# Weight sums on GpSimd, stores through SyncE and conversions at other hooks, in a three-layer kernel on one core

## The chip, the cores and the metric

The kernel runs on one core of a Trainium2 chip. The metric is the device time of one execution in microseconds; less is better. TensorE (PE in the profile) multiplies matrices, VectorE (DVE), ScalarE (ACT) and GpSimd (POOL) work on elements, and SyncE (SP) issues transfers. Each engine runs its own instructions in program order, and semaphores order the engines among each other.

## The reference, cut to what matters

```python
q_s = softmax(q, axis=-1); k_s = softmax(k, axis=2)       # (4, 8, 576, 64)
kv = einsum('bhsd,bhse->bhde', k_s, v)
x = einsum('bhsd,bhde->bhse', q_s, kv)                    # reshaped to (2304, 512)
p = domain_probs / (domain_probs.sum(-1) + 1e-09)         # (2304, 4)
y = sum(p[:, e:e+1] * (relu(x @ w1[e]) @ w2[e]) for e in range(4))   # w1 512x1024, w2 1024x512
h = y @ w_in                                              # 512x2048, float64 in memory
out = elu(h) @ w_out                                      # 2048x512, float64 in memory
```

The outputs are float32. The weights of the last layer arrive as float64.

## The kernel before, in words

The kernel has one long list of matmuls for TensorE, and puts the work of the other engines between them by hand. A matrix product keeps float32 accuracy by splitting each operand in a high and a low part (`hi`, `lo`) and adding three products.

**Stages.** First comes attention for 16 pairs of heads, interleaved from about 23 us on with the first expert (`first`, `second`, matmuls of line 974). From about 272 us the remaining work goes in 30 `STEPS` (s, b): s counts groups of four 128-wide blocks of the hidden layer, b the three blocks of 768 tokens. Steps with s < 6 belong to experts 1 to 3, steps with s from 6 on to the last layer with its ELU. In each step the first layer is done by seven products of sums of quarters instead of eight (`product`, line 1110, twice seven a step). The operands on the token side (`ring_load`, line 688) come from memory through eight ring slots. A slot is loaded in the second half of a step and read in the first half of the next. For s < 5 the second layer is done the same way (`second_product`, line 1254); later steps use plain matmuls (`chunk`, lines 1167 to 1169).

**Weight parts.** Every step group needs two calls of `w1_steps(s, p)`. Each turns a raw weight tile `r` into four pairs of high and low parts: `hi(k)` is a copy on ScalarE (line 734), `lo(k)` a subtraction on VectorE (line 744). `sums1` (lines 748 and 749) and `sums2` (lines 753 and 754) overwrite the raw tile with the sums that later parts need, on VectorE. The order is begin with `hi(0)`, `lo(0)`, `sums1`, `hi(1)`, `lo(1)`, `sums2`, `hi(2)`, `lo(2)`, `hi(3)`, `lo(3)`. There are 20 such parts: two ahead of the first step, then in the last step of one group and the first of the next. When `lo(3)` is done, the buffer of `r` is free for the next weight load (`w_load`).

**Conversions.** `convert` turns one tile of a float64 weight into float32 in 32 runs. The load is issued on SyncE (lines 435 and 437), then come lines 455, 461 and 465 on VectorE, an exponential on ScalarE (468), lines 471 and 474 on VectorE, and the store to a scratch tensor in memory (477), issued on ScalarE. Runs marked `aside` use the tile `gt`, which the fast steps use as well. `w_load` reads the scratch tensor in the last layer.

**Hooks.** What is put between matmuls hangs on numbered hooks. Up to 272 us a hook comes after every 2048 columns of line 974 and runs what `at(n, fn)` put there; before hook 0 the list `START` gives the order by name. In the steps there are 24 hooks a step (`at2`, `tick`), run between products. A conversion at hook t has its load at t - 7 and its instructions at the offsets of its list, spaced 2 (d = 2) or 1 (d = 1).

**Steps behind a product.** After product 0 of a half step ScalarE copies one bank (line 1312), after product 1 another (1314); after products 2 and 4 VectorE adds (1319, 1326). Line 1276 adds a second-layer product to the accumulator. In the ELU steps ScalarE runs lines 1140 to 1142, VectorE 1143 and 1145, ScalarE 1149 and GpSimd 1150. The domain weights `pn` are normalised by `normalise` (lines 605 to 608), four VectorE operations at hook 2; `pn` is first read when expert 0 leaves PSUM (line 1017).

```python
for s, (put, t, d, aside) in enumerate(CONV):
    put(t - 7, lambda s=s, x=aside: convert_load(s, x))
    for n, fn in zip((0, 1, 2, 3, 4, 5, 7) if d == 1 else (0, 2, 4, 6, 10, 12, 16), convert(s, aside)):
        put(t + n, fn)
```

Of the kernel before, what the change touches and what calls it, by code (L numbers as in the profile page):

```python
# [21 lines left out]
def tile_attention_moe_moe(  # L22
# [13 lines left out]
    nc = tc.nc  # L36
# [19 lines left out]
        kvlo2 qmul2 qturn1 x0 qhi1 kcopy3 qturn2 xhi0 qlo1 qhi2 x1 whi1 xhi1 krec3 xlo0 wlo0 qlo2 qturn3 kv3  # L56
        xlo1 qhi3 qlo3 x2 kvhi3 wlo1 xhi2 kvlo3 x3 xhi3 xlo2 xlo3 p0 p1
    """
# [381 lines left out]
    def convert(s, aside):  # L440
# [35 lines left out]
        )  # L476
        yield lambda: nc.scalar.dma_start(out=scratch[s // 2, :, s % 2, :], in_=t["y"])

# [132 lines left out]

    at(2, normalise)

# [101 lines left out]
    def w1_steps(s, p):  # L715
# [27 lines left out]
        def lo(k):  # L743
            tt(out=dst(k, 1), in0=src(k), in1=dst(k, 0).bitcast(F32), op=ALU.subtract)  # L744

# [5 lines left out]
        def sums2():  # L751
            f1, f2 = r[0][:, 0], r[0][:, 1]
            tt(out=f2[:, 2:], in0=f2[:, 2:], in1=f1[:, :2], op=ALU.subtract)
            tt(out=f1[:, 2:], in0=f1[:, 2:], in1=f2[:, 2:], op=ALU.subtract)

        m = int(s >= S_MOE)
        return {
            -5: begin, -4: lambda: lo(0), -2: sums1, -1: lambda: hi(1), 0: lambda: lo(1), 1: sums2,
            4: lambda: hi(2), 5: lambda: lo(2), 8: lambda: hi(3), 10 - m: lambda: lo(3),
        }  # L760
# [72 lines left out]
    end1 = NB * S_FAST * SH  # L833
    CONV = [(at, t, 2, True) for t in (12, 30, 48, 146, 164)]
    CONV += [(later, 34 + 22 * n, 2, False) for n in range(15)]
    CONV += [(later, end1 + 13 + 12 * n, 1, True) for n in range(3)]
    end2 = NB * S_MOE * SH
    CONV += [(later, end2 + 40 + 12 * n, 1, True) for n in range(NCONV - len(CONV))]
    for s, (put, t, d, aside) in enumerate(CONV):
        put(t - 7, lambda s=s, x=aside: convert_load(s, x))  # L840
        for n, fn in zip((0, 1, 2, 3, 4, 5, 7) if d == 1 else (0, 2, 4, 6, 10, 12, 16), convert(s, aside)):
            put(t + n, fn)
# [202 lines left out]
    for step in START.split():  # L1045
        n, i = step[:-1], int(step[-1])
        if n == "whi":
            whi(0, i)
        elif n == "wlo":
            wlo_ahead(0, i)  # L1050
        elif n == "p":
            hidden(0, 0, (i,), 0, EARLY_D)
        elif n == "l":
            early_loads()
        elif n in K_STEPS:
            K_STEPS[n](i, lambda s: bank(early[s]))
        else:
            Q_STEPS[n](i, lambda s: bank(early[s]), (0,))
# [362 lines left out]
```

## Time and profile before

| | us |
|---|---|
| median of 3 runs | 1239.99 (1238.53 to 1240.53) |
| the profiled execution | 1239.69 |
| its span, first to last instruction | 1237.9 |
| TensorE busy | 1194.2 (96%) |
| VectorE busy | 846.2 (68%) |
| ScalarE busy | 635.4 (51%) |
| GpSimd busy | 511.3 (41%) |

The times of the engines are unions of their instructions' spans. Matmuls are pipelined, so a busy TensorE isn't always at its peak. In timelines a number in brackets is the idle time of the engine just before the instruction, with what ended it. "ACTq" and "SPq" are DMA issues by ScalarE's and SyncE's sequencers, not counted as busy. PEclk is the granted TensorE clock as a share of 2.4 GHz; 0.5 is 1.2 GHz.

### The profile page before, as it was taken

To read this page: it belongs to the slowest core of one execution; us is meant where nothing else is said; L and a number is where in the kernel's file an instruction comes from. 1 tells how busy PE (TensorE), PEld (TensorE's weight loads), DVE (VectorE), ACT (ScalarE), POOL (GpSimd) and SP (SyncE) were. 2 spreads that over 40 slices of the span, in tenths; PEclk is the share of its full clock that TensorE was granted. 3 is DMA by queue.
4 is the path that set the end of the run, shared out by engine and by line. 5 is a ranking of instruction groups with operands and counts; after the bars stand their busy time and mean duration, and the time that the engine had idled before them with its cause. 6 is when DMAs were issued, how large, how long until landed. Compare 5 with 4: busy or idle time off the path is not lost.

```text
span 1237.9 us, 20542 instructions
## 1 busy us (share of the span) xinstructions
PE 1194.2 (96%) x7336; PEld 1101.8 (89%) x7336; DVE 846.2 (68%) x1486; ACT 635.4 (51%) x1361; POOL 511.3 (41%) x484
## 2 busy tenths in 40 slices
PE   8699999999999999999999999999999899999998
PEld 7588889888999999999999999888888788999997
DVE  5976887535697688688688687666566677456443
ACT  5454544325455555455455443456676656556552
POOL 3532543006447447447447433335524422422221
PEclk6999999999999999999999999999999999999999
DMA  8444666726666566666666668998976565655541
GB/s 222 143 141 118 218 221 218 273 96 214 221 221 239 221 222 239 246 222 238 228 215 240 234 212 289 342 313 300 336 266 231 194 257 198 226 187 173 182 167 77
DMA packets 155174, 272.32 MB, mean 220 GB/s; under 512 B 12864, under 2 KB 77888, under 8 KB 155072
## 3 DMA queue, kind: packets, MB, share of 16 engines
q1 hardware_dynamic: 145856, 254.23, 59.9%
q10 hardware_dynamic: 9216, 16.78, 3.7%
q8 instruction: 58, 0.95, 0.3%
q14 instruction: 44, 0.36, 0.1%
HBM read 224.83 MB, written 46.14 MB: 219 GB/s over the span
## 4 chain that ended last, share of the span: by engine, by line
PE 72%; DVE 15%; ACT 5%; DMA 4%; issue 3%; POOL 0%; ACTq 0%; SPq 0%; DVEq 0%; POOLq 0%
PE o L1254 14%; PE h L1110 13%; PE m L1110 13%; PE h L974 7%; PE o L974 7%; PE o L1169 5%; PE o L1168 5%; PE o L1167 5%; DVE accB L1276 1%; DVE w1s L744 1%; DMA xl<-xs 1%; PE m L375 1%; DMA xs<-stage 1%; DVE ce L471 1%; DVE r L783 1%
## 5 line engine op out<-in xcount | busy, mean ns | idle before, releaser
L1110 PE MATMUL m<-xh,w1s 128*128 128x384 f32 x840 | 246.5, 339 | 14.8 <-ACT h L1314 7.2
L1110 PE MATMUL h<-xh,w1s 128*128 128x384 f32 x840 | 245.0, 337 | 8.7 <-DVE m L1319 4.5
L1110 PEld LDWEIGHTS m<-xh,w1s 128*128 128x128 f32 x840 | 154.4, 188 | 24.8 <-ACT h L1314 9.3
L1110 PEld LDWEIGHTS h<-xh,w1s 128*128 128x128 f32 x840 | 154.8, 188 | 14.0 <-DVE m L1319 5.6
L1143 DVE SCALAR_TENSOR_TENSOR extra<-extra,half 128x384 f32<-128x384 f32 x96 | 57.5, 599 | 126.1 <-ACT half L1142 126.1
L1110 PE MATMUL h<-xl,w1s 128*128 128x384 f32 x420 | 140.9, 335 | 0.0
L1110 PE MATMUL m<-xl,w1s 128*128 128x384 f32 x420 | 140.8, 335 | 0.0
L974 PE MATMUL o<-w2t,hpa 128*128 128x512 f32 x432 | 118.5, 402 | 1.2 <-DVE hpa L1006 1.0
L974 PE MATMUL h<-xh,w1t 128*128 128x256 f32 (+1 forms) x512 | 113.2, 300 | 0.1
L974 PEld LDWEIGHTS h<-xh,w1t 128*128 128x128 f32 x512 | 87.0, 194 | 5.2 <-POOL w1t L421 0.3
L1254 PE MATMUL o<-w2g,xh 128*128 128x256 f32 x540 | 90.4, 282 | 0.0
L974 PEld LDWEIGHTS o<-w2t,hpa 128*128 128x128 f32 x432 | 76.0, 190 | 15.3 <-DVE hpa L1006 2.9
L1254 PE MATMUL o<-w2g,hpa 128*128 128x256 f32 x540 | 88.9, 282 | 0.0
L1254 PE MATMUL o<-w2g,xl 128*128 128x256 f32 x540 | 87.3, 282 | 0.0
L1110 PEld LDWEIGHTS h<-xl,w1s 128*128 128x128 f32 x420 | 79.2, 189 | 1.5
L1110 PEld LDWEIGHTS m<-xl,w1s 128*128 128x128 f32 x420 | 78.9, 188 | 1.4
L1254 PEld LDWEIGHTS o<-w2g,xh 128*128 128x128 f32 x540 | 78.1, 190 | 0.0
L974 PE MATMUL h<-xl,w1t 128*128 128x256 f32 (+1 forms) x256 | 77.9, 304 | 0.0
L1254 PEld LDWEIGHTS o<-w2g,hpa 128*128 128x128 f32 x540 | 76.2, 190 | 0.0
L1254 PEld LDWEIGHTS o<-w2g,xl 128*128 128x128 f32 x540 | 75.8, 190 | 0.0
L775 POOL TENSOR_TENSOR w2g<-r,w2g 128x512 fp32r<-128x512 f32 x35 | 48.7, 1404 | 59.8 <-ACT w2g L774 59.8
L744 DVE TENSOR_TENSOR w1s<-r,w1s 128x512 fp32r<-128x512 f32 x80 | 68.3, 859 | 4.0 <-ACT w1s L734 4.0
(263 smaller groups left out, 2858.0 us busy)
## 6 DMA issues: line engine op xcount, KB each, us to landing
xh<-xs SPq DMA_DIRECT2D x210, 384.0 KB, 5.7
xl<-xs SPq DMA_DIRECT2D x210, 384.0 KB, 6.2
r<-in_w_dram SPq DMA_DIRECT2D x60, 256.0 KB, 3.9
xs<-stage SPq DMA_DIRECT2D x43, 256.0 KB, 4.1
xs<-xh SPq DMA_DIRECT2D x21, 384.0 KB, 3.8
xs<-xl SPq DMA_DIRECT2D x21, 384.0 KB, 4.2
r<-scratch ACTq DMA_DIRECT2D x28, 256.0 KB, 5.5
gt<-in_w_in_dram SPq DMA_DIRECT2D x9, 512.0 KB, 4.6
```

Of the source, the lines that this page charges most:

```text
L375: nc.tensor.matmul(t[:, a, :HALF], kv[:, l, :], r[:, a, :], start=(n == 0), stop=(n == 2))
L471: yield lambda: dve.scalar_tensor_tensor(out=t["e"], in0=words(U16, 3), scalar=1 << 15, in1=t["e"], op0=ALU.bitwise_and, op1=ALU.bitwise_or)
L744: tt(out=dst(k, 1), in0=src(k), in1=dst(k, 0).bitcast(F32), op=ALU.subtract)
L775: nc.gpsimd.tensor_tensor(out=t[:, 1], in0=src, in1=t[:, 0].bitcast(F32), op=ALU.subtract)
L783: nc.vector.tensor_tensor(out=o, in0=x, in1=y, op=ALU.subtract)
L974: nc.tensor.matmul(out, lhsT, rhs, **kw)
L1110: nc.tensor.matmul(dst, t[:, wl, c + dl, :], x[xl_][:, dl, :], start=(n == 0 and p < 2), stop=(n == 5), skip_group_check=True,)
L1143: nc.vector.scalar_tensor_tensor(out=e_, in0=e_, scalar=1.0, in1=t, op0=ALU.add, op1=ALU.mult)
L1167: nc.tensor.matmul(o, gh, w[:, 0, :], start=(f == 0), stop=False)
L1168: nc.tensor.matmul(o, gh, w[:, 1, :], start=False, stop=False)
L1169: nc.tensor.matmul(o, gl, w[:, 0, :], start=False, stop=(f == FS - 1))
L1254: nc.tensor.matmul(o, l, r, start=(first_write and m == 0 and c != 1), stop=(m == 5), skip_group_check=True)
```

## The change

1. `lo(3)` and both subtractions of `sums2` run on GpSimd instead of VectorE. `hi(2)` and `lo(2)` stand one hook later; `lo(3)` stands one hook earlier for s < 6.
2. The store of a converted tile is issued by SyncE instead of ScalarE, and one hook later (d = 2) or two (d = 1).
3. `normalise` is taken from hook 2 into `START`, ahead of its last entry, so ahead of hook 0.
4. The conversions get other hooks. Before the steps there are eight instead of five, at 30, 50 and 70 (d = 2) and 146, 160, 173, 185, 197 (d = 1). In the fast steps there are 13 at a distance of 26 hooks instead of 15 at 22. Three follow as before, and the last eight (before: nine) stand 12 hooks apart from the same hook on.

```diff
-        xlo1 qhi3 qlo3 x2 kvhi3 wlo1 xhi2 kvlo3 x3 xhi3 xlo2 xlo3 p0 p1
+        xlo1 qhi3 qlo3 x2 kvhi3 wlo1 xhi2 kvlo3 x3 xhi3 xlo2 xlo3 p0 n0 p1
...
-        yield lambda: nc.scalar.dma_start(out=scratch[s // 2, :, s % 2, :], in_=t["y"])
+        yield lambda: nc.sync.dma_start(out=scratch[s // 2, :, s % 2, :], in_=t["y"])
...
-    at(2, normalise)
...
         def lo(k):
-            tt(out=dst(k, 1), in0=src(k), in1=dst(k, 0).bitcast(F32), op=ALU.subtract)
+            eng = nc.gpsimd if k == 3 else nc.vector
+            eng.tensor_tensor(out=dst(k, 1), in0=src(k), in1=dst(k, 0).bitcast(F32), op=ALU.subtract)
...
-            tt(out=f2[:, 2:], in0=f2[:, 2:], in1=f1[:, :2], op=ALU.subtract)
-            tt(out=f1[:, 2:], in0=f1[:, 2:], in1=f2[:, 2:], op=ALU.subtract)
-
-        m = int(s >= S_MOE)
+            nc.gpsimd.tensor_tensor(out=f2[:, 2:], in0=f2[:, 2:], in1=f1[:, :2], op=ALU.subtract)
+            nc.gpsimd.tensor_tensor(out=f1[:, 2:], in0=f1[:, 2:], in1=f2[:, 2:], op=ALU.subtract)
+
         return {
             -5: begin, -4: lambda: lo(0), -2: sums1, -1: lambda: hi(1), 0: lambda: lo(1), 1: sums2,
-            4: lambda: hi(2), 5: lambda: lo(2), 8: lambda: hi(3), 10 - m: lambda: lo(3),
+            5: lambda: hi(2), 6: lambda: lo(2), 8: lambda: hi(3), 9: lambda: lo(3),
         }
...
-    CONV = [(at, t, 2, True) for t in (12, 30, 48, 146, 164)]
-    CONV += [(later, 34 + 22 * n, 2, False) for n in range(15)]
+    CONV = [(at, t, 1 + (t < 100), True) for t in (30, 50, 70, 146, 160, 173, 185, 197)]
+    CONV += [(later, 34 + 26 * n, 2, False) for n in range(13)]
...
-        for n, fn in zip((0, 1, 2, 3, 4, 5, 7) if d == 1 else (0, 2, 4, 6, 10, 12, 16), convert(s, aside)):
+        for n, fn in zip((0, 1, 2, 3, 4, 5, 9) if d == 1 else (0, 2, 4, 6, 10, 12, 17), convert(s, aside)):
...
+        elif n == "n":
+            normalise()
```

## Rows read from the trace of the kernel before

**Rows 1.** Windows by stage: length, busy time (instructions) of PE, PEld, DVE, ACT, POOL; PEclk; DMA share, GB/s
```profile
0.00:62.00 62.00, 47.28 (x312) 39.98 (x313) 46.54 (x102) 33.52 (x80) 28.91 (x40) 0.81 0.65 182
62.00:272.00 210.00, 209.42 (x1442) 184.47 (x1442) 142.79 (x264) 87.51 (x182) 61.57 (x53) 1.00 0.57 189
272.00:754.00 482.00, 470.13 (x3258) 463.32 (x3257) 365.63 (x632) 243.04 (x516) 259.91 (x234) 1.00 0.65 228
754.00:1238.00 484.00, 467.35 (x2330) 414.01 (x2328) 291.23 (x490) 271.36 (x583) 160.89 (x158) 1.00 0.66 230
```
**Rows 2.** Windows by step, fast stage: one undisturbed step, and the sum of eight stalled steps
```profile
387.50:417.20 29.70, 29.70 (x213) 29.70 (x212) 20.93 (x40) 15.36 (x33) 19.22 (x18) 1.00 0.74 277
...
sum 247.92, PE 239.50 PEld 237.20 DVE 198.58 ACT 123.64 POOL 122.00; mean PE 29.94 PEld 29.65 DVE 24.82 ACT 15.46 POOL 15.25
```
**Rows 3.** Timeline ahead of a stall of the fast stage: start, duration, engine, instruction, [idle before]
```profile
440.96 1.23 DVE L753 TENSOR_TENSOR r<-r 128x256 f32<-128x256 f32 x1
...
442.22 0.43 DVE L754 TENSOR_TENSOR r<-r 128x256 f32<-128x256 f32 x1
...
442.57 0.56 DVE L1319 TENSOR_TENSOR m<-h,extra 128x384 f32<-128x384 f32 x1
...
443.18 0.44 PE L1110 MATMUL h<-xh,w1s 128*128 128x384 f32 x1 [1.51 <-DVE m L1319]
```
**Rows 4.** Lines 744, 1319 (ns min/median/max); two GpSimd groups (busy us, mean ns)
```profile
L744 DVE TENSOR_TENSOR w1s<-r,w1s x80: 410/684/1789, 251.5 to 1135.7; 128x512 fp32r<-128x512 f32 x60, 128x256 fp32r<-128x256 f32 x20
...
L1319 DVE TENSOR_TENSOR h<-m,extra x30: 552/559/567, 276.9 to 1189.6; 128x384 f32<-128x384 f32 x30
...
L775 POOL TENSOR_TENSOR w2g<-r,w2g 128x512 fp32r<-128x512 f32 x35 | 48.7, 1404 | 59.8 <-ACT w2g L774 59.8
...
L954 POOL TENSOR_TENSOR accB<-accB 128x256 f32<-128x256 f32 x18 | 15.8, 880 | 6.6 <-DVE stage L948 5.5
```
**Rows 5.** Windows by step, ELU stage: one undisturbed step, and the sum of four disturbed
```profile
1152.20:1183.50 31.30, 31.30 (x158) 28.25 (x157) 15.11 (x26) 16.30 (x37) 8.12 (x8) 1.00 0.56 202
...
sum 136.80, PE 127.81 PEld 111.90 DVE 90.04 ACT 86.53 POOL 46.52; mean PE 31.95 PEld 27.98 DVE 22.51 ACT 21.63 POOL 11.63
```
**Rows 6.** Timeline ahead of a stall of the ELU stage
```profile
978.09 1.66 DVE L474 SCALAR_TENSOR_TENSOR gt<-gt,ce 128x512 f32<-128x512 f32 x1
...
980.18 0.49 ACT L1140 ACTIVATE m<-m 128x384 f32<-128x384 f32 x1 [4.29 <-DVE gt L474]
...
982.99 0.47 ACT L1314 ACTIVATE m<-h 128x384 f32<-128x384 f32 x1 [0.56 <-DVE half L1145]
...
983.52 0.44 PE L1110 MATMUL h<-xh,w1s 128*128 128x384 f32 x1 [1.73 <-ACT m L1314]
```
**Rows 7.** Timeline of the first 62 us, VectorE's lines and the stalls behind them
```profile
32.27 0.21 DVE L605 TENSOR_REDUCE psm<-pn 128x18 f32<-128x72 f32 x1
...
33.87 0.23 DVE L608 TENSOR_TENSOR pn<-pn,psm 128x72 f32<-128x72 f32 x1
...
37.67 0.47 PE L352 MATMUL m<-ident,accA 96*128 96x96 f32 x3 [2.44 <-POOL accA L345]
...
56.41 1.63 DVE L461 TENSOR_SCALAR gt<-gt 128x512 int32<-128x512 int32 x1
...
60.18 0.46 PE L231 MATMUL m<-accB 128*128 128x128 f32 x2 [1.79 <-issue]
```
**Rows 8.** Windows in the first 62 us (columns as in rows 1)
```profile
35.00:40.00 5.00, 2.56 (x15) 2.24 (x15) 3.58 (x8) 2.42 (x6) 3.08 (x4) 0.88 0.90 290
40.00:42.00 2.00, 2.00 (x9) 1.81 (x8) 1.93 (x6) 0.98 (x3) 0.83 (x1) 0.50 0.30 82
```
**Rows 9.** SyncE's longest wait (us, times, longest); line 477's issues (ns min/median/max) and landings
```profile
SPq L688 <- PE h L1110: 342.8, 88, 17.1
...
L477 ACTq DMA_DIRECT2D scratch<-gt x17: 326/327/359, 74.5 to 1027.5; - x17
...
DMA to landing us min/median/max: 2.0/5.1/7.5
```

## The prediction

> **What bounds the kernel now.** The windows by stage come first. TensorE is busy for 1194 of 1238 us, and the rest is spread unevenly: about 15 us of the first 62, nothing between 62 and 272, 12 us of the layer computed by fast products (272 to 754), 17 us after that [rows 1]. VectorE is at 76% in the third stage, ScalarE at 56% and GpSimd at 33% in the fourth. So no other engine is the bound; TensorE is, and time can only come from its stalls. What a stall costs is better read from the length of a step than from the idle time in front of one matmul, because a restarted pipeline costs more. A step of the fast stage without a stall takes 29.70 us; eight steps with one take 247.92 us, 10.3 us more than eight times that [rows 2]. A step of the ELU stage takes 31.30 us undisturbed; the four disturbed ones take 136.80 us, 11.6 us more [rows 5].
>
> Next, the timeline in front of a stall. In the fast stage the same picture returns eight times, once in each step of rows 2: TensorE waits for the addition of line 1319, which VectorE could have started when its product was done, but two subtractions of `sums2` (lines 753 and 754) stand in front. At 441 us they take 1.23 and 0.43 us, and TensorE idles 1.51 us [rows 3]. In the ELU stage it is ScalarE's queue: it reaches the store of a converted tile (line 477), waits 4.29 us for VectorE's last multiplication, which itself took 1.66 us, and only then goes on; the copy of line 1314 is late and TensorE idles 1.73 us [rows 6]. In the first 62 us it is VectorE again [rows 7].
>
> **Part 1, sums and one `lo` to GpSimd.** Removed from VectorE in each of 20 weight parts: `sums2` (two 128x256, 0.43 us when free, 1.66 us together in rows 3) and `lo(3)` (128x512, median 0.68, up to 1.79 us [rows 4]). Added to GpSimd: 1.40 us for `lo(3)` by the same operation at line 775, and twice 0.88 us for `sums2` by the 128x256 one of line 954 [rows 4]: 3.2 us, in all 63 us on an engine that stands at 54% in the stage where it is busiest. In the eight places the removed pair is as long as the stall, or nearly. The gain is bounded by 0 and the 10.3 us; I take 7.5, since other VectorE work stays in the same queue.
>
> New is a wait: ScalarE's `hi(2)` needs what GpSimd subtracts. It stands four hooks later, 5.0 us at 29.70 us per 24 hooks [rows 2]. GpSimd needs 1.8 us, and one operation in front of it up to 1.4 us [rows 4]: 3.2 us, so it should be there. Queued behind `hi(2)` on ScalarE are the relu and copies of the next products. I charge 1 us; 0 and 20 us are the ends (last rival). `hi(2)` and `lo(2)` one hook later, `lo(3)` one earlier, cost nothing: the parts are first read in the next step or half step, five hooks on, about 6 us. The weight load behind `lo(3)` on SyncE waits now for GpSimd instead of VectorE; its cover is the same.
>
> The rows also show a cost: a VectorE operation with two SBUF inputs, median 0.68 us, takes up to 1.79, while line 1319, which reads PSUM, always takes 0.55 to 0.57 [rows 4]. More GpSimd work means more such stretching of what stays on VectorE. I charge 2 us for it, together with the conversions meeting other work at their new hooks; ends 0 and 7.5. The Trainium skill (SBUF — State Buffer, Who interferes with whom) says that an instruction of VectorE with two SBUF inputs and one of GpSimd that reads SBUF exclude each other, the later one waiting for the other's end. It speaks against moving work to GpSimd; the trace agrees on which lines stretch, and what it would make of the time is the second rival.
>
> **Part 2, the store through SyncE.** Moved: 32 issues, 0.33 us each on ScalarE's queue [rows 9], and the wait in front of each. SyncE issues the ring loads too, so they now stand behind a store that waits for VectorE. But SyncE spends its time waiting for TensorE to free ring slots (343 us [rows 9]), a slot is filled in the second half of a step and read half a step (about 15 us) later, and the store's place is five hooks (spacing 2) or four (spacing 1) behind the last multiplication. A delay of 2 to 4 us is covered. On ScalarE the four steps of rows 5 hold 11.6 us: bounds 3.0 (nine issues of 0.33) and 11.6. In rows 6 ScalarE could have started line 1140 some 4 us earlier; line 1314 then waits for VectorE's line 1145, which stands behind the same multiplication, so not all comes back. I take 8.5, nearer the upper end because in these rows the wait is thirteen times the issue. The staging tile `gt` is rewritten about four hooks (5 us) after the store's place, and a store lands in 2.0 to 7.5 us, median 5.1 [rows 9]: a possible new wait of VectorE for a landing. SyncE mostly issues ahead of its place; I charge 0.5 us, ends 0 and 5.
>
> The Trainium skill (DMA: Bandwidth & Descriptors, Issuing engines are not separate DMA queues) says that transfers issued by several engines share the DMA engines, so that spreading them saves issue time alone. By that the store's part would be the lower bound, 3.0 us; the trace differs, in that the wait in front of the issue is the larger.
>
> **Part 3, normalising earlier.** Four small VectorE operations run from 32.27 to 34.10 us, 1.8 us, in front of work that TensorE waits for 2.44 us at 37.7 us [rows 7]. Placed ahead of hook 0 they fall in a stretch where VectorE is nearly idle. Gain about 1.3 us of the 2.44 (the chain behind is shorter by 1.8 us, less 0.5 for an operation of VectorE that then meets more of GpSimd's); ends 0 and 1.8. The clock was at half speed for about 3.4 us there (0.88 of 35 to 40, 0.50 of 40 to 42, a little after), following a stretch with TensorE busy for 2.56 of 5 us [rows 8]. If the shorter stall spares that, 1.7 us more comes back; I leave it to the range.
>
> **Part 4, conversions at other hooks.** The first one no longer falls at 52 to 71 us: its line 461 took 1.63 us in front of the work behind the 1.79 us stall at 60.2 us [rows 7]. I take 1.6 us, ends 0 and 3 (two such operations). Three more go to hooks 146 to 206, in the stage where TensorE never idles and VectorE is at 68% [rows 1]; cost nothing, ends 0 and 2 if VectorE's relu parts come late. That leaves 13 instead of 15 in the fast stage and 8 instead of 9 after it, at the same hooks.
>
> **Sum.** The profiled execution took 1239.69 us (span 1237.9, 1.8 around it), 0.3 below the median 1239.99. 1239.7 - 7.5 - 8.5 - 1.3 - 1.6 + (1 + 2 + 0.5) = 1224.3 us. With every gain at its upper end and no charge: 1239.7 - 10.3 - 11.6 - 1.8 - 3 - 1.7 = 1211; I do not expect all together.
>
> **Rivals.**
> 1. The store's move is worth little: ScalarE's next work waits for VectorE anyway. For it: line 1314 waits for line 1145 in rows 6. Against it: line 1140 needs no VectorE and started 4.29 us late. 3.0 instead of 8.5: 1229.8 us.
> 2. The shared port gives the gain back: in the eight places one VectorE operation is stretched by about 0.6 us (half of 1.79 - 0.68). 5 of 7.5 us lost: 1229.3 us. Against it: the removed operations were the stretched ones.
> 3. The stalls only move: another queue entry stops TensorE at the same steps, and the first stage alone keeps its 2.9 us against 3.5 of charges: 1240 us. Against it: the spare time of every other engine in rows 1.
> 4. Slower: ScalarE's `hi(2)` waits for GpSimd. GpSimd itself waits for ScalarE's outputs in order, and in 20 weight parts a wait may fall on ScalarE in front of a copy that TensorE needs. At 1 us each, with no gain from part 1: 1239.7 - 8.5 - 2.9 + 20 = 1248.3 us. It decides from about 0.6 us each (11.4 / 20). Against it: 5.0 us of distance for 3.2 us of work.
>
> That the change does not do what it says is hardly possible: the engine and the hook of each instruction are written out.
>
> **Numbers.** Chances: forecast 0.45 (alone 1218 to 1229), rival 1 0.20, rival 2 0.17, rival 3 0.07, rival 4 0.11. Predicted 1224. The range goes from 1216, where some of the upper ends and the clock come in, to 1240, which holds rivals 1 to 3; outside are rival 4 and a few in 100 below. A measurement of this kernel tells about 0.2% (2.5 us) from no change. Faster 0.82, same 0.07, slower 0.11.
>
> **What would show it.** Right: no VectorE line between a finished product and line 1319 in the eight places, these steps at 30.0 us or less; no wait of ScalarE for line 474, the ELU steps near 32 us; TensorE busy a few us longer in the first 62; GpSimd about 60 us busier. Wrong: ScalarE idle in front of line 734 until GpSimd is done; SyncE waiting for line 474 with ring loads late; VectorE idle until a store lands.

## The result and the profile after

Six runs of each kernel, side by side: 1231.2 us with the change (1225.5 to 1232.9), 1240.3 us before (1237.1 to 1242.9). The ratio is 0.9918, with a 95% interval of 0.9892 to 0.9944: faster by 0.8%. The prediction said 1224.0, in a range of 1216 to 1240. The profiled execution has a span of 1229.4 us, 8.5 less than before, and is the one that took 1231.2 us.

The windows by stage, with the columns and bounds of [rows 1]:

```profile
0.00:62.00 62.00, 48.28 (x328) 40.66 (x328) 44.57 (x103) 34.80 (x84) 31.01 (x40) 0.83 0.63 178
272.00:754.00 482.00, 475.31 (x3294) 469.37 (x3292) 342.64 (x592) 245.41 (x521) 292.73 (x270) 1.00 0.65 230
754.00:1238.00 484.00, 460.22 (x2280) 407.92 (x2280) 289.08 (x456) 266.19 (x573) 184.44 (x180) 0.99 0.64 223
...
sum 1238.00, PE 1193.26 PEld 1102.57 DVE 826.88 ACT 635.24 POOL 572.82; mean PE 298.32 PEld 275.64 DVE 206.72 ACT 158.81 POOL 143.21
```

GpSimd went up to 572.8 us from 511.3 (the sum of its column over the whole span), the 60 us that were moved to it. In the stage of the fast products TensorE now idles 6.7 us instead of 11.9, and 1.8 of the 6.7 already belong to step 16, which begins at 742.4. The last stage has a new figure: its granted clock is 0.99 instead of 1.00, so TensorE spent more time at the lower of its two levels than before.

Since the stages shift, steps are compared by their lengths, from the first product of one step (line 1111, before 1110) to that of the next in the timeline. The fence has windows with such bounds: the eight steps of [rows 2] (the sum), step 16, the four steps of [rows 5] (the sum).

```profile
sum 238.20, PE 237.71 PEld 237.03 DVE 178.27 ACT 121.26 POOL 144.08; mean PE 29.71 PEld 29.63 DVE 22.28 ACT 15.16 POOL 18.01
...
742.40:783.10 40.70, 36.07 (x173) 32.09 (x172) 19.58 (x32) 13.12 (x26) 8.86 (x8) 0.92 0.71 241
...
sum 132.40, PE 127.17 PEld 112.30 DVE 91.54 ACT 85.90 POOL 58.03; mean PE 31.79 PEld 28.08 DVE 22.89 ACT 21.47 POOL 14.51
```

The eight stalled fast steps took 247.9 us and take 238.2, which leaves 0.6 us of 10.3. The four disturbed ELU steps took 136.8 and take 132.4. But step 16, the first after the fast products, took 33.0 us before (754.1 to 787.2) and now takes 40.7. This one step gives back nearly half of what the others gain. (The bounds of windows are rounded to 0.1 us, so a window and a step of the table can differ by that.)

| us, profiled execution | before | after | difference |
|---|---|---|---|
| start of step 0 | 271.8 | 269.5 | -2.3 |
| steps 1 to 15 | 459.8 | 450.5 | -9.3 |
| step 16 | 33.0 | 40.8 | +7.8 |
| steps 17 to 19 | 103.0 | 102.6 | -0.4 |
| steps 20 to 24 | 168.2 | 164.1 | -4.1 |
| step 25 to the end | 179.5 | 179.7 | +0.2 |

**What stalls step 16.** The timeline of the kernel after, SyncE's issues first, then VectorE's lines and the matmul that was late:

```profile
739.35 0.69 DVE L474 SCALAR_TENSOR_TENSOR gt<-gt,ce 128x512 f32<-128x512 f32 x1
...
739.35 0.33 SPq L435 DMA_DIRECT2D gt<-in_w_in_dram  x1
...
741.15 1.68 SPq L687 DMA_DIRECT2D xl<-xs  x1
745.70 0.32 SPq L477 DMA_DIRECT2D scratch<-gt  x1
...
752.83 1.19 DVE L461 TENSOR_SCALAR gt<-gt 128x512 int32<-128x512 int32 x1 [6.67 <-DMA scratch<-gt]
754.05 1.63 DVE L465 SCALAR_TENSOR_TENSOR gt<-gt 128x512 f32<-128x512 uint32 x1
...
756.27 0.55 DVE L1320 TENSOR_TENSOR h<-m,extra 128x384 f32<-128x384 f32 x1
...
756.87 0.69 PE L1111 MATMUL m<-xh,w1s 128*128 128x384 f32 x1 [4.63 <-DVE h L1320]
```

The converted tile is finished by line 474 at 740.04. Its store, line 477, goes out at 745.70, behind the load of the next conversion and four ring loads. It lands 7.1 us later, at 752.80, and only then may VectorE write the tile again (line 461), after 6.67 us of waiting. Line 1320 stands behind that in VectorE's queue, and TensorE idles 4.63 us for it. Lines 461 and 465 are also slow here: 1.19 and 1.63 us, where p2_store_alone (below) has 0.43 and 0.69 for the same conversion.

Why the store is late by 5.7 us is in the waits (engine, line waited for: total us, times, longest):

```profile
SPq L477 <- DMA gt<-in_w_in_dram: 2.8, 1, 2.8
...
DVE gt L461 <- DMA scratch<-gt: 12.5, 5, 6.7
...
ACT w1s L733 <- POOL r L753: 4.6, 2, 2.5
```

SyncE could have issued the store at 742.83, when the ring load of 741.15 was issued, but waited 2.8 us more for the load of the next conversion to land (745.64). (The 2.8 us before 742.83 went with the five issues in front of it.) The store has nothing to do with that load's data; in the trace's semaphore records it signals its end on the same semaphore as the load, and waits for that to be free. There the program hands eight semaphores round, in its own order, to the DMAs of SyncE and ScalarE together; between this load and this store stand four ring loads and three weight loads that ScalarE issues. The kernel before has such waits too. There ScalarE issues the stores, and ring loads on SyncE wait for two of them to land:

```profile
SPq L688 <- DMA scratch<-gt: 7.8, 2, 6.0
```

VectorE's waits for landed stores came to 12.5 us in all, where the kernel before has a row of 3.5 us (2 times). The last row of the fence with the waits after the change belongs to rival 4 and is taken up below.

The idle stretch has a second price. Windows behind it (columns as before, granted clock third from the end):

```profile
755.00:758.00 3.00, 1.13 (x4) 1.13 (x5) 2.96 (x6) 0.00 (x0) 1.81 (x2) 0.71 0.00 0
758.00:760.00 2.00, 2.00 (x8) 2.00 (x8) 1.76 (x3) 0.00 (x0) 0.00 (x0) 0.50 0.53 115
760.00:762.00 2.00, 2.00 (x7) 1.81 (x6) 0.00 (x0) 0.87 (x2) 0.00 (x0) 0.50 0.96 333
762.00:764.00 2.00, 2.00 (x8) 1.52 (x8) 0.00 (x0) 0.00 (x0) 0.00 (x0) 0.73 0.84 335
764.00:766.00 2.00, 2.00 (x12) 1.87 (x11) 1.12 (x2) 0.08 (x1) 0.00 (x0) 1.00 0.01 3
```

After the 4.63 us without a matmul the clock stood at half (1.2 of 2.4 GHz) until about 763: 7 or 8 matmuls in 2 us, then 12. From 756.9 on that loses about 3.1 us, an estimate: half of the 6.2 us from the matmul's start to 763.1, where the clock returns. 4.6 + 3.1 = 7.7 us, the whole excess of step 16.

### The profile page after: what moved, and what is told of

Its sections match the earlier page's. It is cut to its first block, busy times and chain, and to the rows that moved or that the text cites. A ratio compares the mean times of both kernels' runs of the same rounds, so it can differ in the third digit from the quotient of the medians.

```text
span 1229.4 us, 20602 instructions
## 1 busy us (share of the span) xinstructions
PE 1193.3 (97%) x7336; PEld 1102.6 (90%) x7336; DVE 826.9 (67%) x1426; ACT 635.2 (52%) x1361; POOL 572.8 (47%) x544
## 4 chain that ended last, share of the span: by engine, by line
PE 74%; DVE 11%; DMA 6%; ACT 3%; issue 3%; POOL 1%; SPq 1%; DVEq 0%; ACTq 0%; POOLq 0%
PE o L1255 16%; PE h L1111 14%; PE m L1111 14%; PE o L973 7%; PE h L973 7%; PE o L1170 5%; PE o L1169 5%; PE o L1168 5%; DMA scratch<-gt 2%; PE m L283 1%; PE m L375 1%; DMA r<-in_w_dram 1%; DMA xh<-xs 1%; DMA xs<-stage 1%; DVE r L782 1%
## 5 line engine op out<-in xcount | busy, mean ns | idle before, releaser
L1144 DVE SCALAR_TENSOR_TENSOR extra<-extra,half 128x384 f32<-128x384 f32 x96 | 61.3, 639 | 114.7 <-ACT half L1143 114.6
L1004 ACT ACTIVATE hpa<-h 128x256 fp32r<-128x256 f32 (+1 forms) x64 | 26.0, 406 | 70.9 <-PE h L973 70.8
L744 DVE TENSOR_TENSOR w1s<-r,w1s 128x512 fp32r<-128x512 f32 (+1 forms) x60 | 54.5, 908 | 10.8 <-ACT w1s L733 10.8
```

The lines of the kernel that those rows point to most:

```text
L744: eng.tensor_tensor(out=dst(k, 1), in0=src(k), in1=dst(k, 0).bitcast(F32), op=ALU.subtract)
L1004: nc.scalar.activation(out=gh, in_=h, func=AF.Relu)
L1144: nc.vector.scalar_tensor_tensor(out=e_, in0=e_, scalar=1.0, in1=t, op0=ALU.add, op1=ALU.mult)
```

## The experiments

The first four kernels make one part of the change each, on the kernel before. The next four keep all of it and alter the place of the store or the conversions around step 16. The last four take the store and the sums apart further. Ratios are to the kernel before on the same chip; step lengths are from each kernel's profiled execution.

### p1_sums_alone: part 1 on the kernel before

```diff
-            tt(out=dst(k, 1), in0=src(k), in1=dst(k, 0).bitcast(F32), op=ALU.subtract)
+            eng = nc.gpsimd if k == 3 else nc.vector
+            eng.tensor_tensor(out=dst(k, 1), in0=src(k), in1=dst(k, 0).bitcast(F32), op=ALU.subtract)
...
-            tt(out=f2[:, 2:], in0=f2[:, 2:], in1=f1[:, :2], op=ALU.subtract)
-            tt(out=f1[:, 2:], in0=f1[:, 2:], in1=f2[:, 2:], op=ALU.subtract)
+            nc.gpsimd.tensor_tensor(out=f2[:, 2:], in0=f2[:, 2:], in1=f1[:, :2], op=ALU.subtract)
+            nc.gpsimd.tensor_tensor(out=f1[:, 2:], in0=f1[:, 2:], in1=f2[:, 2:], op=ALU.subtract)
...
-            4: lambda: hi(2), 5: lambda: lo(2), 8: lambda: hi(3), 10 - m: lambda: lo(3),
+            5: lambda: hi(2), 6: lambda: lo(2), 8: lambda: hi(3), 9: lambda: lo(3),
```

> The kernel before with part 1 alone (sums2 and lo(3) on GpSimd, with the hooks that go with it). Theory (the fast stage gained because of part 1): steps 1 to 15 fall from 459.8 us to about 451, steps 20 to 24 stay within 2 us of 168.1, the time is about 1231. Rival (the fast stage gained because two conversions left it and the others moved): steps 1 to 15 stay above 456 and the time above 1236.

Measured: 1232.2 us (1230.5 to 1233.6), ratio 0.9933, interval 0.9914 to 0.9953. Steps 1 to 15 take 450.5 us, to the tenth what the whole change gives them; step 16 takes 33.0. Steps 20 to 24 take 170.4 us, 2.2 more than before. So the gain in the fast steps is all of part 1, and the stall of step 16 is not of its making.

### p2_store_alone: part 2 on the kernel before

```diff
-        yield lambda: nc.scalar.dma_start(out=scratch[s // 2, :, s % 2, :], in_=t["y"])
+        yield lambda: nc.sync.dma_start(out=scratch[s // 2, :, s % 2, :], in_=t["y"])
...
-        for n, fn in zip((0, 1, 2, 3, 4, 5, 7) if d == 1 else (0, 2, 4, 6, 10, 12, 16), convert(s, aside)):
+        for n, fn in zip((0, 1, 2, 3, 4, 5, 9) if d == 1 else (0, 2, 4, 6, 10, 12, 17), convert(s, aside)):
```

> The kernel before with part 2 alone (store through SyncE, later offsets). Theory (the late store makes VectorE wait until it has landed): step 16 grows from 33.0 us to between 36 and 41, steps 20 to 24 fall from 168.1 to about 164, the time stays between 1238 and 1242. Rival (the stall of step 16 belongs to the new hooks of the conversions): step 16 stays at 33, steps 20 to 24 fall to about 164, the time is about 1236.

Measured: 1241.6 us (1236.1 to 1245.4, 10 runs), ratio 1.0011, interval 0.9991 to 1.0031: no gain. In the profiled execution, with 1238.0 us one of the shorter, steps 20 to 24 fall by 3.4 to 164.8 us, while steps 1 to 15 and step 16 lose 1.1 and 1.0. The time and steps 20 to 24 came as the theory said, the stall did not: step 16 takes 34.0 us, not 36 to 41. VectorE's waits in this kernel, then its timeline in step 16:

```profile
DVE gt L461 <- DMA scratch<-gt: 12.5, 6, 6.0
```

```profile
763.79 0.43 DVE L461 TENSOR_SCALAR gt<-gt 128x512 int32<-128x512 int32 x1 [6.00 <-DMA scratch<-gt]
...
766.14 0.44 PE L1110 MATMUL m<-xh,w1s 128*128 128x384 f32 x1 [0.71 <-DVE h L1319]
```

The same 12.5 us of waiting for landed stores as after the change. The part takes ScalarE's wait away and puts one on VectorE. In step 16 that wait is 6.00 us long, nearly as long as after the change, and TensorE idles only 0.71 us for it. Here it ends 8.2 us after the start of the step, after the change 10.5. So the late store is needed for the long stall (without part 2 step 16 takes 33.1 us, e9_without_part2), but alone, in this execution, it does not make it. Which of the other parts adds what is missing was not tried. Nor does this trace show what the median execution lost, which took 3.6 us more than the profiled one.

### p3_hooks_alone: part 4 on the kernel before

```diff
-    CONV = [(at, t, 2, True) for t in (12, 30, 48, 146, 164)]
-    CONV += [(later, 34 + 22 * n, 2, False) for n in range(15)]
+    CONV = [(at, t, 1 + (t < 100), True) for t in (30, 50, 70, 146, 160, 173, 185, 197)]
+    CONV += [(later, 34 + 26 * n, 2, False) for n in range(13)]
```

> The kernel before with part 4 alone (conversions at other hooks). Theory: step 0 starts about 1.3 us earlier, steps 1 to 15 change by less than 3 us, step 16 stays near 33 us, the time is about 1238. Rival (the stall of step 16 belongs to the new hooks): step 16 reaches 37 us or more and the time is 1240 or more.

Measured: 1237.0 us (1234.0 to 1238.3), ratio 0.9977, interval 0.9965 to 0.9990. Step 0 starts 1.2 us earlier, step 24, which has lost its conversion, is 1.3 shorter (31.3), steps 1 to 15 are 1.2 longer, and step 16 takes 33.0: the hooks alone do not stall it.

### p4_normalise_alone: part 3 on the kernel before

```diff
-    at(2, normalise)
...
-        xlo1 qhi3 qlo3 x2 kvhi3 wlo1 xhi2 kvlo3 x3 xhi3 xlo2 xlo3 p0 p1
+        xlo1 qhi3 qlo3 x2 kvhi3 wlo1 xhi2 kvlo3 x3 xhi3 xlo2 xlo3 p0 n0 p1
...
+        elif n == "n":
+            normalise()
```

> The kernel before with part 3 alone (normalising ahead of hook 0). Theory: the stall at 37.7 us comes 1 to 2 us earlier or shrinks, step 0 starts about 1.3 us earlier than 271.8, the time is about 1238.7. Rival (the next wait of the first stage takes it back): step 0 starts within 0.4 us of 271.8.

Measured: 1239.5 us (1237.7 to 1241.8), ratio 1.0002, interval 0.9990 to 1.0014: nothing. One line of the kernel before, and then the timeline of this kernel, to be read against [rows 7]:

```profile
34.50 0.73 PE L974 MATMUL o<-w2t,hpa 128*128 128x512 f32 x2 [0.72 <-DVE hpa L1006]
```

```profile
25.31 0.22 DVE L605 TENSOR_REDUCE psm<-pn 128x18 f32<-128x72 f32 x1
...
34.37 0.47 PE L352 MATMUL m<-ident,accA 96*128 96x96 f32 x3 [2.44 <-POOL accA L345]
...
45.55 0.44 PE L352 MATMUL m<-ident,accA 96*128 96x96 f32 x3 [3.49 <-POOL accA L328]
...
58.98 0.46 PE L231 MATMUL m<-accB 128*128 128x128 f32 x2 [1.90 <-issue]
```

The four operations run 7 us earlier, as intended. They had stood in front of VectorE's line 1006, and the 0.72 us for which TensorE waited there are gone; they had also stood in front of lines 322 to 339, which GpSimd's line 345 waits for. From line 974's matmul at 29.81 us (here at 27.50) to the one behind line 345 the kernel before takes 7.9 us, this one 6.9. The 2.44 us in front of that matmul stay 2.44, since TensorE arrives earlier as well. The other 2.3 us by which this execution is ahead at that point are not the change's: its clock is at half level from 8.4 to 22.1 us, in the kernel before from 8.1 to 28.6. The stall behind, at 45.55 us, is 3.49 us long and was 2.32 at 46.40. At 58.98 the kernel is 1.2 us ahead, and a stretch at half clock (0.72 on average from 58 to 64 us, 1.00 before) takes that back: step 0 starts at 271.8 in both, as the rival said.

### e5_store_on_scalar: all of the change, but the store goes out by ScalarE, at the new hooks

```diff
-        yield lambda: nc.sync.dma_start(out=scratch[s // 2, :, s % 2, :], in_=t["y"])
+        yield lambda: nc.scalar.dma_start(out=scratch[s // 2, :, s % 2, :], in_=t["y"])
```

> Everything of the change stays, the store alone goes back to ScalarE at its new, later hook. Theory (the stall of step 16 comes from SyncE's queue: there the store stands behind the next conversion's load and goes out 5.7 us late): step 16 falls from 40.8 to 33 to 34 us and TensorE has no gap of over 2 us in it; steps 20 to 24 go back from 164.1 to 167 to 170 us, since ScalarE waits again for the last multiplication in front of the store; steps 1 to 15 stay at 450.5; time 1226 to 1230. Rival (the landing before the tile is rewritten is what costs, whichever engine issues the store, because its hook is later): step 16 stays at 38 us or more and the time is 1234 to 1238.

Measured: 1222.4 us (1221.3 to 1222.6), ratio 0.9867, interval 0.9844 to 0.9889. Step 16 is back at 33.1 us, as the theory said; the rival falls. But steps 20 to 24 did not go back to 167 or more: they take 162.0, better than with SyncE. Timeline around the store of step 16's beginning:

```profile
739.33 0.69 DVE L474 SCALAR_TENSOR_TENSOR gt<-gt,ce 128x512 f32<-128x512 f32 x1
...
740.06 0.37 ACTq L477 DMA_DIRECT2D scratch<-gt  x1
...
747.28 0.43 DVE L461 TENSOR_SCALAR gt<-gt 128x512 int32<-128x512 int32 x1 [0.86 <-DMA scratch<-gt]
```

ScalarE issues 0.04 us after line 474's end, so the tile is free at 747.3 instead of 752.8. The lesson of the miss is that the later hook does what was put down to the engine: at the new place ScalarE mostly finds line 474 done (it waits for it 6.3 us in 3 places; in the kernel before, 30.1 us in 12).

### e6_store_early: all of the change, the store of spacing 1 at offset 5

```diff
-        for n, fn in zip((0, 1, 2, 3, 4, 5, 9) if d == 1 else (0, 2, 4, 6, 10, 12, 17), convert(s, aside)):
+        for n, fn in zip((0, 1, 2, 3, 4, 5, 5) if d == 1 else (0, 2, 4, 6, 10, 12, 17), convert(s, aside)):
```

> Everything of the change stays, but with spacing 1 the store through SyncE is put at offset 5, right behind the last multiplication and ahead of the next conversion's load, instead of offset 9. Theory: it no longer stands behind that load, goes out within 2 us of the multiplication and lands about 5 us later, before the tile is rewritten: VectorE's waits for a landing fall from 12.5 us in all to 4 or less, step 16 falls from 40.8 to 33 to 34 us, steps 20 to 24 stay at 162 to 165; time 1221 to 1225. Rival (VectorE's rewriting is too near whatever the offset): waits of 8 us or more stay, step 16 at 38 or more, time 1229 to 1232.

Measured: 1223.6 us (1221.0 to 1224.9), ratio 0.9873, interval 0.9850 to 0.9896. Step 16 takes 33.0 us, steps 20 to 24 take 162.6, and no wait of line 461 for a store is left. As expected, with one price: now the next load stands behind a store that waits for VectorE, and line 455 waits for loads.

```profile
DVE ce L455 <- DMA gt<-in_w_out_dram: 4.0, 4, 1.5
```

### e7_store_behind_load: all of the change, the store of spacing 1 at offset 6

```diff
-        for n, fn in zip((0, 1, 2, 3, 4, 5, 9) if d == 1 else (0, 2, 4, 6, 10, 12, 17), convert(s, aside)):
+        for n, fn in zip((0, 1, 2, 3, 4, 5, 6) if d == 1 else (0, 2, 4, 6, 10, 12, 17), convert(s, aside)):
```

> Everything of the change stays, but with spacing 1 the store through SyncE is put at offset 6, just behind the next conversion's load (offset 5), instead of 9. Theory (the store is held by the landing of that load, whose semaphore it reuses): it is issued only 5 to 6 us after the load even though it stands one place behind it, so step 16 stays at 38 to 41 us and the time at 1229 to 1232. Rival (the three hooks of delay and the ring loads between are what makes it late): it goes out about 2 us after the multiplication, step 16 is 33 to 34 us, time 1221 to 1225.

Measured: 1220.8 us (1220.4 to 1223.4), ratio 0.9857, interval 0.9836 to 0.9879, the lowest of all, and 10 us below the change as it was made. Here the theory, as it was put, fell. Of this kernel the timeline (SyncE's issues, VectorE's line 461), then SyncE's wait in the waits, then windows of step 16 and of steps 20 to 24:

```profile
739.34 0.33 SPq L435 DMA_DIRECT2D gt<-in_w_in_dram  x1
...
740.71 0.38 SPq L477 DMA_DIRECT2D scratch<-gt  x1
...
745.90 0.32 SPq L687 DMA_DIRECT2D xl<-xs  x1
...
749.40 0.43 DVE L461 TENSOR_SCALAR gt<-gt 128x512 int32<-128x512 int32 x1 [3.00 <-DMA scratch<-gt]
```

```profile
SPq L687 <- DMA gt<-in_w_in_dram: 2.8, 1, 2.8
```

```profile
742.40:775.40 33.00, 33.00 (x173) 29.66 (x172) 18.79 (x31) 13.21 (x26) 9.24 (x8) 1.00 0.87 302
877.70:1039.00 161.30, 158.06 (x782) 140.41 (x782) 114.12 (x176) 105.33 (x229) 69.01 (x61) 1.00 0.68 247
```

The store is behind the same load, and goes out at 740.71, not at 745.70. The wait of 2.8 us for that load's landing is still there, but a ring load has it. In both kernels it is the sixth issue counted from the load, and in e6_store_early the sixth from the store waits for the store. So which transfer is held goes by its position in the order in which the semaphores are handed out and not by what it moves, and a ring load has time where the store has none. Rival and theory each had half: the ring loads between make the store late, because they push it to the place that waits.

### e8_space_20: all of the change, the conversions around step 16 spaced by 20 hooks

```diff
-    CONV += [(later, end1 + 13 + 12 * n, 1, True) for n in range(3)]
+    CONV += [(later, end1 + 13 + 20 * n, 1, True) for n in range(3)]
```

> Everything of the change stays, but the three conversions around step 16 stand 20 hooks apart instead of 12; the last eight are as they were. Theory: the store is as late as before but the tile is rewritten eight hooks (about 10 us) later, so VectorE does not wait for a landing there: step 16 is 33 to 35 us instead of 40.8, steps 20 to 24 stay near 164, time 1223 to 1226. Rival (step 16 is long because of what the steps hold there, not because of the spacing): the 7 us move to step 17 or 18 and the time stays at 1229 to 1232.

Measured: 1227.9 us (1226.9 to 1230.7), ratio 0.9914, interval 0.9891 to 0.9936: between the two expectations. Step 16 takes 33.1 us, as the theory said, but step 17 takes 39.5 instead of 35.0, as the rival said. Timeline and windows there:

```profile
795.52 0.68 DVE L474 SCALAR_TENSOR_TENSOR gt<-gt,ce 128x512 f32<-128x512 f32 x1
...
797.57 0.55 DVE L1120 SCALAR_TENSOR_TENSOR xl<-h,xl 128x384 fp32r<-128x384 f32 x1
...
798.17 0.44 PE L1111 MATMUL h<-xh,w1s 128*128 128x384 f32 x1 [1.94 <-DVE xl L1120]
```

```profile
799.00:801.00 2.00, 2.00 (x7) 1.71 (x6) 0.47 (x2) 0.80 (x2) 0.03 (x1) 0.56 0.92 361
801.00:803.00 2.00, 2.00 (x7) 1.54 (x7) 0.00 (x0) 0.00 (x0) 1.42 (x2) 0.59 1.03 343
```

The third of these conversions now falls in step 17, where VectorE also runs the subtractions of line 947, the low parts of the last layer's operands. Line 1120 comes late behind it, TensorE idles 1.94 us, and half clock follows. It is another stall than that of step 16, so the spacing does remove the wait, and the place that it moves work to has none to spare.

### e9_without_part2: the change without its second part

```diff
-        yield lambda: nc.sync.dma_start(out=scratch[s // 2, :, s % 2, :], in_=t["y"])
+        yield lambda: nc.scalar.dma_start(out=scratch[s // 2, :, s % 2, :], in_=t["y"])
...
-        for n, fn in zip((0, 1, 2, 3, 4, 5, 9) if d == 1 else (0, 2, 4, 6, 10, 12, 17), convert(s, aside)):
+        for n, fn in zip((0, 1, 2, 3, 4, 5, 7) if d == 1 else (0, 2, 4, 6, 10, 12, 16), convert(s, aside)):
```

> The change without its second part: the store is issued by ScalarE at its old hooks (offsets 7 and 16), parts 1, 3 and 4 stay. Theory (what lengthens the ELU steps is that ScalarE reaches the store before VectorE's last multiplication is done, so that the hook is what counts and not the engine): ScalarE issues within 0.1 us of that multiplication's end nearly every time, steps 20 to 24 go back from 162.0 (ScalarE at the later hooks) to 166 to 170 us, step 16 is 33 to 34, steps 1 to 15 stay at 450.5; time 1226 to 1230. Rival (with the weight sums gone from VectorE the multiplication comes early enough for the old hooks): steps 20 to 24 stay at 161 to 163 us and the time at 1221 to 1223.

Measured: 1229.0 us (1229.0 to 1230.5), ratio 0.9929, interval 0.9914 to 0.9943. Steps 20 to 24 take 169.2 us and step 16 takes 33.1, as the theory said; steps 1 to 15 take 451.9, 1.4 more than it said. One of the stalls of steps 20 to 24 in the timeline, and behind it ScalarE's largest wait for line 474 in the waits:

```profile
912.28 1.74 POOL L744 TENSOR_TENSOR w1s<-r,w1s 128x512 fp32r<-128x512 f32 x1
912.79 1.78 DVE L744 TENSOR_TENSOR w1s<-r,w1s 128x512 fp32r<-128x512 f32 x1
914.49 0.68 DVE L474 SCALAR_TENSOR_TENSOR gt<-gt,ce 128x512 f32<-128x512 f32 x1
...
915.20 0.33 ACTq L477 DMA_DIRECT2D scratch<-gt  x1
...
915.58 0.42 ACT L733 ACTIVATE w1s<-r 128x256 fp32r<-128x256 f32 x1 [3.83 <-DVE r L748]
...
919.70 0.69 PE L1111 MATMUL m<-xh,w1s 128*128 128x384 f32 x1 [2.50 <-ACT h L1315]
```

```profile
ACT m L1141 <- DVE gt L474: 12.3, 4, 4.3
```

Two `lo` subtractions run beside each other on GpSimd and VectorE, 1.74 and 1.78 us long where VectorE's median is 0.68; VectorE's ends 0.55 us after GpSimd's. Line 474 comes late, ScalarE sits at the store, and 3.83 us of its time are gone. The same pair stands in p1_sums_alone, at 914.85 and 915.37 us. There TensorE idles 2.49 us behind it, where the kernel before idles 1.15 at this place, and 3.4 us at half clock follow, worth about 1.7. In the kernel before the same row of waits is 12.1 us in 4, and five more bring all of ScalarE's waits for line 474 to 30.1 us in 12; with the change none is left. Against this kernel, e5_store_on_scalar and e7_store_behind_load are 6.6 and 8.2 us faster (the kernel before took 1238.5 and 1238.6 us beside them), and their steps 20 to 24 7.2 and 7.9 us shorter: that is what the second part is worth beside the others, when the store does not run late.

### e10_hooks_of_store: the kernel before, the store on ScalarE at the new hooks

```diff
-        for n, fn in zip((0, 1, 2, 3, 4, 5, 7) if d == 1 else (0, 2, 4, 6, 10, 12, 16), convert(s, aside)):
+        for n, fn in zip((0, 1, 2, 3, 4, 5, 9) if d == 1 else (0, 2, 4, 6, 10, 12, 17), convert(s, aside)):
```

> The kernel before with one edit: the store stays on ScalarE and stands at the change's later hooks (offsets 9 and 17 instead of 7 and 16). Theory: ScalarE no longer waits for the multiplication in most places; steps 20 to 24 fall from 168.2 to 163 to 166 us with step 16 at 33 to 34, so the time is 1234 to 1237, where both the engine and the hook moved gave 1241. Rival (the engine is needed as well, the wait only moves on to another entry of ScalarE's queue): steps 20 to 24 stay at 167 to 170 us, time 1238 to 1241.

Measured: 1235.9 us (1233.9 to 1238.5), ratio 0.9983, interval 0.9973 to 0.9993. Steps 20 to 24 take 164.0 us instead of 168.2, step 16 takes 33.0. The hook alone, with no change of engine, gives what the theory expected; with the engine changed as well the gain was gone (p2_store_alone, 1.0011 with an interval of 0.9991 to 1.0031).

### e11_sums2_alone and e12_lo3_alone: part 1 in two halves

```diff
-            tt(out=f2[:, 2:], in0=f2[:, 2:], in1=f1[:, :2], op=ALU.subtract)
-            tt(out=f1[:, 2:], in0=f1[:, 2:], in1=f2[:, 2:], op=ALU.subtract)
+            nc.gpsimd.tensor_tensor(out=f2[:, 2:], in0=f2[:, 2:], in1=f1[:, :2], op=ALU.subtract)
+            nc.gpsimd.tensor_tensor(out=f1[:, 2:], in0=f1[:, 2:], in1=f2[:, 2:], op=ALU.subtract)
...
-            4: lambda: hi(2), 5: lambda: lo(2), 8: lambda: hi(3), 10 - m: lambda: lo(3),
+            5: lambda: hi(2), 6: lambda: lo(2), 8: lambda: hi(3), 10 - m: lambda: lo(3),
```

> The kernel before with the two subtractions of sums2 on GpSimd and hi(2), lo(2) one hook later; lo(3) stays on VectorE. Theory (these two stood in front of the addition that TensorE waits for): steps 1 to 15 fall from 459.8 to 450 to 452 us, as with the whole of part 1; time 1231 to 1233. Rival (lo(3) off VectorE is what lets the addition come in time): steps 1 to 15 stay at 456 to 460 us, time 1236 to 1240.

The other half is `lo(3)` through `eng` as in p1_sums_alone, with `9: lambda: lo(3)`, and nothing else.

> The kernel before with lo(3) alone on GpSimd, one hook earlier for the early units; sums2 stays on VectorE. Theory: lo(3) stood in front of nothing that TensorE waits for, so steps 1 to 15 stay at 458 to 460 us and steps 20 to 24 at 167 to 170; time 1238 to 1240. Rival: steps 1 to 15 fall by 4 us or more, time 1232 to 1236.

Measured: `sums2` alone 1231.8 us (1228.9 to 1234.5), ratio 0.9948, interval 0.9927 to 0.9968; `lo(3)` alone 1242.7 us (1240.7 to 1245.8), ratio 1.0031, interval 1.0016 to 1.0046. Windows of steps 1 to 15 and 20 to 24, first of the kernel with `sums2` moved, then of the one with `lo(3)` moved (there steps 20 to 24 come first):

```profile
295.70:746.80 451.10, 447.74 (x3152) 444.84 (x3152) 343.36 (x591) 229.84 (x488) 263.94 (x244) 1.00 0.67 236
882.50:1049.60 167.10, 160.20 (x782) 141.65 (x781) 111.61 (x185) 106.48 (x230) 61.32 (x57) 0.99 0.67 244
```

```profile
887.60:1058.90 171.30, 160.58 (x781) 141.62 (x780) 113.48 (x189) 106.41 (x230) 61.38 (x53) 0.99 0.65 239
292.40:752.00 459.60, 448.55 (x3151) 444.54 (x3151) 345.35 (x601) 229.61 (x488) 260.24 (x234) 1.00 0.66 231
```

`sums2` brings 8.7 of the 9.3 us in the fast steps. `lo(3)` brings 0.2 there and its steps 20 to 24 are 3.1 us longer, more than the expectation had. In both traces 3.4 us of steps 20 to 24 are at half clock, worth about 1.7 us; the kernel before has none there. The ratio of `lo(3)`, over seven runs, says that moving it is a loss on the kernel before. The best placing of the store together with `sums2` alone was not tried.

## Why the prediction was right, and by how much it was not

The sign and the range were right. The point was 7.2 us too low. One step failed by about as much; the misses of the other terms nearly cancel, and that is luck.

**Part 1 (7.5, bounds 0 to 10.3): right, 9.3.** The stalls that [rows 3] show are the two subtractions in front of the addition; without them steps 1 to 15 fall by 9.3 us, and `sums2` does nearly all of it. That `lo(3)` would help as well was not argued from a stall, and it does not.

**The charge for `hi(2)` (1 us) and rival 4: no loss.** ScalarE does wait for `sums2` on GpSimd, but only twice, 2.5 us and 2.1 us, at 256.9 and 275.0 us, around the first step, and step 0 takes 22.4 us against 22.5. From step 1 on there is no such wait, so the four hooks of distance were enough.

**The shared port (2 us, ends 0 to 7.5): right in size, in part by luck, and in the ELU steps.** With part 1 alone, steps 20 to 24 grow by 2.2 us, and a stretch at half clock, which no term held, is about 1.7 us of what step 21 loses. The mechanism is in e9_without_part2 and p1_sums_alone: two subtractions side by side, both near 1.8 us, in front of line 474. This agrees with the rule of the Trainium skill (SBUF — State Buffer, Who interferes with whom) that the prediction named, that such instructions exclude each other. The rule's rival, a loss of 5 us or more, did not come.

**Part 2 (8.5, bounds 3.0 to 11.6): right for what it takes away, wrong in its reason.** ScalarE's waits for line 474 are gone, and beside the other parts that is worth 7.2 to 7.9 us of steps 20 to 24 when the store does not run late. In the change itself these steps fell by 4.1 us. But the prediction argued with the engine. The runs show that either edit alone is enough: ScalarE at the later hook, 162.0 us; SyncE at an early place, 161.3 and 162.6; ScalarE at the old hook, 169.2. (SyncE at the old hook itself was not run.) Both together, as in the change, gave 164.1 and the stall of step 16. Rival 1 (3.0 us) falls: the wait in front of the issue was the larger part, as the prediction had it. By the rule of the Trainium skill named there (DMA: Bandwidth & Descriptors, Issuing engines are not separate DMA queues), only issue time is saved. From ScalarE's old hook these runs do not agree: SyncE at an early place saves 6.6 and 7.9 us, and nine issues of 0.33 are 3.0. From ScalarE's later hook they do, since there SyncE saves at most 0.7.

**The landing (0.5 us, ends 0 and 5): the step that failed.** Of the three signs that the prediction gave for being wrong, the last one came, and cost time: VectorE idle until a store lands. (ScalarE idle for GpSimd came twice, as above. SyncE waited 37.3 us for line 474, in 10 places, but TensorE waited for no ring load.) The prediction saw that `gt` is rewritten about four hooks (5 us) after the store's place and that a store lands in 2.0 to 7.5 us [rows 9], and dismissed it with "SyncE mostly issues ahead of its place". It had counted what stands behind the store in SyncE's queue, and not what stands ahead of it: with spacing 1 the new offset 9 is behind the next conversion's load at offset 5 and its ring loads, and the sixth of these issues waits for the first to land. The 7.8 us of SyncE's waits for ScalarE's stores, in the kernel before, show the same kind of wait. So the store went out 5.7 us late, landed 7.1 us after that, and the measured price was 7.8 us in step 16 against the 0.5 charged: 4.6 of idle TensorE and 3.1 at half clock, the second of which no term held. 7.8 less 0.5 is 7.3 us, as much as the distance between 1224.0 and 1231.2, but that is luck. The late stores also cost 1.5 to 2.8 us in steps 20 to 24 (164.1 against 161.3 to 162.6), part 3 gave 1.3 less than forecast, and part 1 gave 1.8 and part 4 about 1.3 more. With the store three hooks earlier the kernel takes 1220.8, below the forecast. And the long stall is the late store's together with the rest of the change, since in p2_store_alone step 16 takes 34.0 us. Rivals 2 to 4 are not what happened: the sums kept their gain, the stalls went, and `hi(2)` waited twice, at no cost.

**Part 3 (1.3): nothing in the time.** The four operations did stand in front of the chain that ends with GpSimd's line 345, and this stretch became 1.0 us shorter without them. But the 2.44 us from which the gain was to come stayed, since TensorE came earlier too, and the next wait (for line 328, 3.49 us instead of 2.32) and the clock took the gain back. What stands behind the wait had not been looked at.

**Part 4 (1.6): more, some 2.9** (0.0023 of 1239 us; by the interval 1.2 to 4.3). Step 0 starts 1.2 us earlier: the stalls at 53.3 and 60.2 us fall from 2.03 and 1.79 to 0.35 and 0.24 us, while one at 46.4 grows from 2.32 to 3.25. These stretches lie at half clock for different times in each trace, so the start of step 0 is better compared over many: it is at 271.2 to 273.1 in the six traces without parts 3 and 4, and at 268.8 to 270.8 in the six with both. That step 24 would lose its conversion, worth 1.3 us, was not in the sum. The 1.2 us that the hooks alone cost in the fast steps does not show beside part 1, where these steps take the same 450.5 us with and without the new hooks.

Open: the change's six runs go from 1225.5 to 1232.9 us, and those of p2_store_alone from 1236.1 to 1245.4. Whether the store's lateness differs from one execution to the next can't be seen, since each kernel has one trace. For the same reason step lengths may hold a stretch at half clock (1.7 us) that another execution doesn't have.

## What to carry to other kernels

A DMA that waits for a result holds everything behind it on its issuing engine, so look first whether it stands too early: moving it a few hooks later, or to an idle queue, is worth the wait and not the issue time. But do one of them, and count from the result to the landing: what stands ahead of it in the new queue, with which earlier transfer it shares a semaphore, how long it flies, and when its buffer is written again. When work goes to a second engine, move only the operations that stand in front of a bound one (here `sums2`), since the others (`lo(3)`) may cost more on the shared path than they free.

## What had not been expected of the hardware

In SyncE's queue an issue can wait for the landing of an earlier DMA that it has no data in common with, because the program gave both the same semaphore: at the start of step 16 the sixth issue counted from the load, 2.8 us on the store in the kernel after, 2.8 us on a ring load when the store stood earlier. And TensorE's clock fell to half after a stall in the middle of the kernel, where [rows 1] have 1.00: for 6.8 us after 4.63 us of idleness in step 16, and for 3.4 us after the 1.94 us of e8_space_20, the 2.49 us of p1_sums_alone and the 2.50 us of e9_without_part2. Such a stall can cost more than itself. It does not always: the kernel before has one of 2.50 us (at 965.7) and e8_space_20 one of 2.90 us (at 984.9) without a fall, so the length of the stall alone does not tell.
